# Scores of one head pair beside the running sums from chunk 3 on, in a single-core attention and MLP kernel with a written-out order

## The chip, the core and the metric

The kernel runs on one core of a Trainium2 chip. The metric is the device time of one execution in microseconds (us). In this text PE is TensorE, DVE is VectorE, ACT is ScalarE, POOL is GpSimd and SP is SyncE, the engine that issues most of the DMAs. PSUM is the memory that PE writes its results to; it has banks of 512 fp32 numbers in each of 128 partitions.

## The reference

Everything is float32, with batch B = 4, heads H = 8, sequence S = 768 and head size D = 48. First a gated recurrence, then a layer norm and a two-layer MLP with a residual:

```python
for t in range(S):
    state = alpha[:, :, t, :, None] * state + einsum('bhd,bhe->bhde', k[:, :, t], v[:, :, t])
    y[:, :, t] = einsum('bhd,bhde->bhe', q[:, :, t], state)
...
x = y.transpose(0, 2, 1, 3).reshape(B, S, 384)
xn = (x - mean(x)) / sqrt(var(x) + 1e-06) * g_ln
out = x + maximum(xn @ w_ch1, 0.0) @ w_ch2          # 384 -> 1536 -> 384
```

The three inputs of the MLP arrive on the chip as 64-bit floats and are rounded to float32 there, by DVE and ACT.

## The kernel before

**Work items.** The sequence is cut into six chunks of 128 steps. One item is one chunk `c` of one batch `b`, with all eight heads, held as four pairs `p` of two heads `i`. The generator `attention(c, b)` computes one item, from loads to the normalised and transposed rows of the MLP's input:

- ACT takes the logarithm of alpha into `la` (L308). PE multiplies it by a triangle of ones to get running sums of the logarithms, in the first 384 columns `lps[:, :DM]` of a PSUM bank (chunk 0 at L313; later by `running_sums`, L288, for most items ahead of time at L403, among the scores of an earlier item). ACT takes exponentials of them (L320, L321), and DVE multiplies keys and queries by those (L323, L325).
- DVE transposes them in blocks (L362), and DMAs through DRAM (`tr`, `td`) bring the transposed keys and queries `kT` and `qT`.
- Scores: PE multiplies `kT` and `qT` (L401), 64 x 64 for each head and each half `s` of the chunk. DVE copies the scores that a triangular mask lets through into `at` (`copy_predicated`, L413).
- State: PE multiplies keys and values into `sums` (L428); DVE adds the old state (L441) and POOL multiplies by the gate (L443), once for each half of the chunk: the tile `mid`, then `st`, which the next chunk of the same batch reads.
- Output `y`: PE adds what comes from the state (L459) and from the scores (L463) in two PSUM banks `yps`. ACT copies one to `x` (L486), DVE adds the other and sums the row for the mean (L489).
- ACT does the layer norm in several short steps (L502 to L515); PE transposes `xn` (L522), and ACT copies that to `xT` (L524). For the last two chunks DMAs do the transposes. The row `x` goes to DRAM for the residual (L498) and comes back later in `ob` (L545).

**The split.** For chunks from `SPLIT` on, the scores of pair 3 go to other places than those of pairs 0 to 2: into the last 128 columns of the bank that holds another item's running sums (`beside`, L389), and in each of the two halves of partitions that the other pairs leave free at that time. So there are two masked copies of 384 and 128 columns, pair 3's part of `y` lands in the opposite banks, and assembling `x` takes two copies by ACT (L474, L476) and two sums by DVE (L479, L482); the mean is made by L502 instead of L504, and `vx`, the values with their halves exchanged, is loaded in three parts instead of two (L153). The matmuls are the same in number and size.

**The MLP.** Chunk 0 is multiplied plainly (`hidden` L558, `project` L570). For chunks 1 to 5 both layers are done with fewer block products than blocks: 15 for the first layer (`hidden_product`, PE at L848, taken out of PSUM by DVE, ACT and POOL at L856 to L891) and 20 for the second (`product`, PE at L674, taken out at L684 to L734). Sums of blocks that these products need are made by DVE (`combine_first`, `combine_weights` L634, `combine_x` L825, `combine_hidden` L661).

**The order.** Nothing is scheduled by a planner. Each of these parts is a Python generator, and a `yield` ends one step of it. The string `ORDER` (L33) gives, letter by letter, which generator takes its next step:

```python
for turn in ORDER:
    next(turns[turn], None)
```

The letters `a` to `x` are the items, four to a chunk in the order of the batches, so `a` to `d` are chunk 0, `m` to `p` chunk 3, `q` to `t` chunk 4 and `u` to `x` chunk 5. `A` to `L` round the weights; `Y`, `Z`, `P` and `Q` are the MLP of chunk 0; `1` and `2` are the first layer's block products, `M` the second layer's, `N`, `S`, `W` and `X` the sums of blocks, `R` and `U` the relus, `O` the loads of rows back. Every engine executes what it was given in this order, and semaphores, which are set by the framework from the tiles that are read and written, hold an instruction until what it needs is there. Six PSUM banks (tag `bank`) serve scores, running sums, `yps`, transposes and products in turn.

Of the kernel before, what the change touches and what calls it, by code (L numbers as in the profile page):

```python
# [19 lines left out]
STAGED = 3  # L20
BY_DMA = 2
X_BY_DMA = 4
SPLIT = 4
AHEAD = 2
G = 32
SCORES = ((0, 0), (0, 1), (1, 0), (1, 1), (3, 0), (2, 0), (3, 1), (2, 1))
# [4 lines left out]


ORDER = (  # L33
    "bacabcadaacbcaadbcadabcababbebaccbadbaaBbccaedcbceAeeaaacbfecfBcdafddeaedbdeafae"
    "bcdccbfgadhAdcgCcdbebeebfhggdfgbfffbCdcgfgecdfchgdfhgabcddchdhAiiegjhacehedhhjfg"
    "biAdfidAeBhBijffYYiCjZZYYifZYlZCgjYDlYYjjZZYBZYgDieEgDgDjZZekEhZYGZgZigZGeeYgYgg"
    "fZYEhfGfkChihiYFYijfgEhgkhFZYhgYfghijgkFeZZlGZShfZYHlhHfYFYZeZHelYiZgllPmZkJIgJk"
    "PeiYjJIflHeSZIQgkIlYSjiPkffennSQlOKjLSnSjmSQhKnSjLnKPkiljnhSQnLkkjkWknkShOmPhkhl"
    "kOOhWlmmphmQmkmXjWQnXjlSQjPmkilXSXkP2OXWjXQjkjW2iXoSWX2oWX22Pi2mnol1j1mom2omSpoo"
    "l1XSpk2oW2m112p1m2pm11m1W211pp12O122r22jnn21lpnmnjSml1riOn2l12Rl111kqS1m21W1Rkp2"  # L40
    "o21mUXpq1mU2rUrnmj1rl2Rno2oomqonrormpokO1rNM2Mipin1op1ionoqUM2qp2W12RkMmNqiMoRtk"
    "UrpkqNM1NoMliMlNUMMNMNMKNqMlNorMWrnmtltNRMsqppMWNMriMMMpNlsqqqnoqttNttMtMsXMMssM"
    "sMNMNMX1oXXppMvstM2MXMMNMsppXoMXoqMsMMXM1nqqv11Xq1trMq2tqX21rn12v1r2ur2r222rvsqs"
    "svsu1rs1nuvvt2s11ss11p22rtsvosn2uropuXru222221uts212stnU1211u1121222Op1Rp2tRU21R"
    "Us1pXqU11x2tO2MM1vwMUM12xuRvu1vurNNNNwtOuuMwRxvNtxRNutwwMM2MOwNXwMNuXMMtNM1rMMMw"
    "qtXMMMxNUNxtMMsNMMMxXxMtXtrMMqMNrMXNvutMMwNuMMMNMMMxMLMOM11vvuq2X2O2wMus1wX11222"
    "2r2Xt1222w22utsqxvw2x2ww1vx21sX12121xwvq2O2x2w111u1uvU121w12s1wuRvx12U11J1q21R1U"
    "OvRxU121wMMu2xxsRNMw2NNMRM1MUNN2MMuUMqXN1MrNNRMNvMXNXMMMM2MMMxNM1uNXMMNMNMOXMXMv"
    "MMXOMMMXxNxwxMMvNMMMMMXMx21w1x222212v12w222x122w2212X11UX2212121121121wx111MU11X"
    "2RR2v1211212211R1URU211XOUM2XNRX1MX1RM2MXN2MXNXNMXXMXMMMN111U1MN1M1122MNM1MM2MM1"  # L50
    "11NNN121O11NM1MM21N1112N1122M1MMM12MM12N222M22M2RM1M2N22MM2MU1ON2M22M2UURR22RNNM"
    "MNM1MMOMRMNMUUM2ONMNNNMO2MMMUMNMMMMMRMMNNMMMNMNMMNMMMMMMMMNMNMMMMMMM"
)


# [1 line left out]
def kernel(  # L57
# [68 lines left out]
    def load(c, m, names):  # L126
# [12 lines left out]
        if "v" in names:  # L139
# [4 lines left out]
            if c:  # L144
# [4 lines left out]
                parts = ((0, 0, NP, NP), (1, 0, NP, 0))  # L149
                if c >= SPLIT:  # L150
                    parts = ((0, 0, NP, NP - 1), (1, 0, NP - 1, 0), (1, NP - 1, 1, H - 1))
# [142 lines left out]
    def attention(c, b):  # L294


        whole, last = c == 0, c + 1 == NCB
        split = c >= SPLIT
        if whole and b % 2 == 0:
# [660 lines left out]
```

## Time and profile before

| what | value |
|---|---|
| median of 3 runs | 421.56 us (421.01 to 423.45) |
| profiled execution | 420.14 us |
| its span (first to last instruction) | 418.3 us |
| PE busy | 409.8 us, 98% |
| DVE busy | 351.4 us, 84% |
| ACT busy | 177.5 us, 42% |
| POOL busy | 151.6 us, 36% |
| bytes moved by DMA | 61.26 MB, 146 GB/s in the mean |
| granted clock of PE | 1.00 |

The times of single lines come from the profiled execution, whose span lies 1.8 us below its own time and whose time lies 1.4 us below the median. A busy share is a mean over the whole span: whether an engine has room has to be read from windows. An engine's busy time counts instructions, which can overlap one another at their ends, so the distance from start to start can be less than a duration.

### The profile page before, as it was taken

Reading aid. Unit: us, or ns where it says so; the run is one execution under the profiler, and the core shown is the slowest. Engines: PE = TensorE matmul, PEld = TensorE weight load, DVE = VectorE, ACT = ScalarE, POOL = GpSimd, SP = SyncE. Lnnn points to the kernel's source line nnn. Section 1 sums busy time; section 2 is a strip of 40 time slices with the busy share of each in tenths; the row PEclk is TensorE's granted clock in tenths of the full one; section 3 lists DMA queues with packets and bytes.
Section 4 is the critical chain, followed back from the end, with each engine's and each line's share of the span. In section 5 each row is a group of like instructions: output and inputs, shape, how many; then the busy total and the mean of one; then the engine's idle time right before and its main releaser. Section 6 shows DMA issues by size and latency. Waiting matters only on the chain.

```text
span 418.3 us, 11560 instructions
## 1 busy us (share of the span) xinstructions
PE 409.8 (98%) x4608; PEld 361.3 (86%) x4608; DVE 351.4 (84%) x713; ACT 177.5 (42%) x440; POOL 151.6 (36%) x164
## 2 busy tenths in 40 slices
PE   7998999999999999999999999999999999999996
PEld 5787888766578889998889999889998899999996
DVE  4999999999999989996888995688876767977873
ACT  5598447724243496414546603364313242014110
POOL 1011000003203980043395033493152940499123
PEclk9999999999999999999999999999999999999999
DMA  8999999987888778587684546433035200001201
GB/s 278 340 302 288 235 196 306 270 184 195 193 233 175 207 153 193 123 203 179 135 213 85 130 102 162 88 96 78 0 116 102 67 0 2 1 19 40 94 20 56
DMA packets 135037, 61.26 MB, mean 146 GB/s; under 512 B 90908, under 2 KB 131100, under 8 KB 134984
## 3 DMA queue, kind: packets, MB, share of 16 engines
q1 hardware_dynamic: 134440, 60.37, 56.1%
q8 instruction: 36, 0.59, 0.6%
q10 hardware_dynamic: 544, 0.17, 0.2%
q14 instruction: 17, 0.14, 0.1%
HBM read 43.12 MB, written 17.39 MB: 145 GB/s over the span
## 4 chain that ended last, share of the span: by engine, by line
PE 89%; DVE 4%; DMA 2%; ACT 2%; issue 1%; POOL 0%; POOLq 0%; SPq 0%; DVEq 0%
PE hps L848 31%; PE ops L674 30%; PE ops L570 8%; PE hps L558 7%; PE aps L401 3%; PE yps L459 2%; PE yps L463 2%; PE sums L428 2%; DMA vn<-in_v_dram 2%; PE xps L522 1%; PE aps L393 1%; DMA ra<-in_alpha_dram 1%; PE lps L313 1%; DVE w L217 1%; PE tps L351 1%
## 5 line engine op out<-in xcount | busy, mean ns | idle before, releaser
L690 POOL TENSOR_TENSOR ob<-ob,u 128x192 f32<-128x192 f32 x40 | 26.2, 665 | 64.5 <-DVE ob L687 48.3
L848 PE MATMUL hps<-sum,w 128*128 128x256 f32 x192 | 46.3, 381 | 0.0
L898 ACT ACTIVATE hT<-hT 128x512 f32<-128x512 f32 x48 | 28.7, 622 | 35.0 <-POOL hT L870 18.5
L443 POOL TENSOR_TENSOR mid<-mid,gate 112x192 f32<-112x192 f32 x20 | 11.6, 580 | 81.8 <-DVE mid L441 51.3
L674 PE MATMUL ops<-w,hT 128*128 128x192 f32 x224 | 40.5, 327 | 0.0
L848 PEld LDWEIGHTS hps<-sum,w 128*128 128x128 f32 x192 | 36.1, 190 | 5.0
L674 PEld LDWEIGHTS ops<-w,hT 128*128 128x128 f32 x224 | 37.1, 190 | 0.7 <-issue 0.2
L848 PE MATMUL hps<-xT,w 128*128 128x256 f32 x136 | 34.0, 380 | 0.0
L570 PE MATMUL ops<-w,hT 128*128 128x384 f32 x96 | 33.0, 492 | 0.0
L558 PE MATMUL hps<-xT,w 128*128 128x256 f32 x144 | 32.5, 382 | 0.0
L558 PEld LDWEIGHTS hps<-xT,w 128*128 128x128 f32 x144 | 27.0, 190 | 4.2
L674 PE MATMUL ops<-ws,sum 128*128 128x192 f32 x160 | 28.7, 327 | 0.0
L848 PEld LDWEIGHTS hps<-xT,w 128*128 128x128 f32 x136 | 25.5, 190 | 3.1
L570 PEld LDWEIGHTS ops<-w,hT 128*128 128x128 f32 x96 | 17.5, 190 | 10.8 <-DVE w L232 0.4
L674 PEld LDWEIGHTS ops<-ws,sum 128*128 128x128 f32 x160 | 26.5, 190 | 0.3
L684 DVE TENSOR_TENSOR ob<-ops,ob 128x192 f32<-128x192 f32 x50 | 17.2, 351 | 10.6 <-PE ops L674 6.5
L443 POOL TENSOR_TENSOR st<-st,gate 112x192 f32<-112x192 f32 x16 | 11.6, 725 | 35.6 <-DVE st L441 25.9
L674 PE MATMUL ops<-ws,hT 128*128 128x192 f32 x128 | 23.6, 328 | 0.0
L459 PEld LDWEIGHTS yps<-st,qT 48*64 48x64 f32 x320 | 19.9, 134 | 4.0 <-issue 2.3
L463 PE MATMUL yps<-vx,at 64*64 64x48 f32 x320 | 22.7, 219 | 0.0
L401 PEld LDWEIGHTS aps<-qT,kT 48*64 48x64 f32 x576 | 19.1, 134 | 4.1 <-issue 0.8
L459 PE MATMUL yps<-st,qT 48*64 48x48 f32 x320 | 22.0, 220 | 0.6 <-ACT x L486 0.6
(248 smaller groups left out, 1131.6 us busy)
## 6 DMA issues: line engine op xcount, KB each, us to landing
ws<-in_moe_w_ch_dram SPq DMA_DIRECT2D x12, 768.0 KB, 5.8
td<-tr SPq DMA_DIRECT2D x64, 96.0 KB, 2.8
vn<-in_v_dram SPq DMA_DIRECT2D x12, 384.0 KB, 6.9
kept<-x SPq DMA_DIRECT2D x24, 192.0 KB, 3.0
ob<-kept SPq DMA_DIRECT2D x24, 192.0 KB, 3.0
out_dram<-ob SPq DMA_DIRECT2D x19, 192.0 KB, 1.9
ra<-in_alpha_dram SPq DMA_DIRECT2D x16, 192.0 KB, 2.6
kT<-td SPq DMA_DIRECT2D x32, 96.0 KB, 3.4
```

Source lines behind the costliest of these rows:

```text
L401: nc.tensor.matmul(to, kT[rs, p, s], qT[rs, p, s], start=True, stop=True)
L428: nc.tensor.matmul(up[h, p], qk_of(c, b)[ts, 1, p, i, :h.stop - h.start], vn[ts, i, p], start=True, stop=True)
L443: nc.gpsimd.tensor_mul(new, new, by)
L459: nc.tensor.matmul(yps[i][halves[s], i, p], qT[rs, p, s], (now, mid)[s][rs, p], start=True, stop=r != i)
L463: nc.tensor.matmul(yps[r][halves[s], i, p], at[halves[r], p, s], by, start=r != i, stop=True)
L558: nc.tensor.matmul(hps, w1[:, j // 2, f, j % 2 * P:][:, :P], xT_of[0][:, f, bs], start=(f == 0), stop=(f == NF - 1))
L570: nc.tensor.matmul(ops_of[b], hT_of[c][:, j, b], w2[:, j], start=(j == 0), stop=(j == NJ - 1))
L674: nc.tensor.matmul(acc, lhs[:, j], rhs[:, j], start=(j == 0), stop=(j == NT - 1))
L684: nc.vector.tensor_add(x, acc, x)
L690: getattr(nc.gpsimd, f"tensor_{op}")(x, x, y)
L848: nc.tensor.matmul(acc[:, i], w, b, start=True, stop=True)
L898: nc.scalar.activation(out=x, in_=x, func=AFT.Relu)
```

## The change

`SPLIT` goes from 4 to 3, so the four items `m` to `p` of chunk 3 are split like those of chunks 4 and 5, and the string `ORDER` is another one from its first letters on, with each letter as often as before. The instructions that come and go: four more masked copies on DVE (L413, 384 and 128 columns in place of 512), four more sums on DVE (L479 and L482 in place of L489), four more copies on ACT (L474 and L476 in place of L486), four L502 in place of L504, and two more loads of `vx`. Matmuls and bytes stay the same.

The diff, with the string cut to the first and last lines that change and those where chunk 3 is worked on:

```diff
@@ -20,7 +20,7 @@
 STAGED = 3
 BY_DMA = 2
 X_BY_DMA = 4
-SPLIT = 4
+SPLIT = 3
 AHEAD = 2
...
 ORDER = (
-    "bacabcadaacbcaadbcadabcababbebaccbadbaaBbccaedcbceAeeaaacbfecfBcdafddeaedbdeafae"
...
-    "kOOhWlmmphmQmkmXjWQnXjlSQjPmkilXSXkP2OXWjXQjkjW2iXoSWX2oWX22Pi2mnol1j1mom2omSpoo"
-    "l1XSpk2oW2m112p1m2pm11m1W211pp12O122r22jnn21lpnmnjSml1riOn2l12Rl111kqS1m21W1Rkp2"
-    "o21mUXpq1mU2rUrnmj1rl2Rno2oomqonrormpokO1rNM2Mipin1op1ionoqUM2qp2W12RkMmNqiMoRtk"
-    "UrpkqNM1NoMliMlNUMMNMNMKNqMlNorMWrnmtltNRMsqppMWNMriMMMpNlsqqqnoqttNttMtMsXMMssM"
...
-    "MNM1MMOMRMNMUUM2ONMNNNMO2MMMUMNMMMMMRMMNNMMMNMNMMNMMMMMMMMNMNMMMMMMM"
+    "abcbacaacdacdabababacbcaabcdadbcbcccbecabaaaedebbaefcafBadbedcefdbadeefcegdbgfdB"
...
+    "kWOlkWOlQmpSXmimiPmWXmlXPkpiQnookjSSXQPSX1jmiSXkS1Xklk1jXKW2Wj22QXW1jSjjk11mnOm1"
+    "oWn2lm2opoo2o2olnmj2mpm1il212Wp22l2122pj12W12pki1O2kmimUmjmn1p2Xnn1kq112ok1n2nk1"
+    "2XlO1m1q2irp122112m2opllRRUWorUpmR1o2MrrqrNrUUi1im2rllo2pMrM1otMl1RooRMpnNMlqqNp"
+    "1UNpMoqqnMN1omNtMplMnNpqpMNoMMNWpmrRMNoMsWOMqMNMMn2moMmrNqsNortqqqt1tMnttsssoqXt"
...
+    "MOMMMNR2RUNMMRMNUMNNNNMMMMMMMMN2MUMMMNOMNMNMMNMMMMMMNMMMNMMMMNMMMMMM"
 )
```

The code that the new value of `SPLIT` reaches in chunk 3 is L150 to L151 (loads of `vx`), L383 to L389, L397 to L404 and L412 to L416 (scores and their copies), L458 to L464 (`y`), L470 to L492 (`x`) and L501 to L504 (the mean).

More of the change, by code (lines that the diff above doesn't have):

```diff
@@ L33 @@
 ORDER = (
-    "bacabcadaacbcaadbcadabcababbebaccbadbaaBbccaedcbceAeeaaacbfecfBcdafddeaedbdeafae"
[L35 to L38, printed above, removed]
-    "kOOhWlmmphmQmkmXjWQnXjlSQjPmkilXSXkP2OXWjXQjkjW2iXoSWX2oWX22Pi2mnol1j1mom2omSpoo"
@@ L40 @@
-    "l1XSpk2oW2m112p1m2pm11m1W211pp12O122r22jnn21lpnmnjSml1riOn2l12Rl111kqS1m21W1Rkp2"
-    "o21mUXpq1mU2rUrnmj1rl2Rno2oomqonrormpokO1rNM2Mipin1op1ionoqUM2qp2W12RkMmNqiMoRtk"
-    "UrpkqNM1NoMliMlNUMMNMNMKNqMlNorMWrnmtltNRMsqppMWNMriMMMpNlsqqqnoqttNttMtMsXMMssM"
-    "sMNMNMX1oXXppMvstM2MXMMNMsppXoMXoqMsMMXM1nqqv11Xq1trMq2tqX21rn12v1r2ur2r222rvsqs"
-    "svsu1rs1nuvvt2s11ss11p22rtsvosn2uropuXru222221uts212stnU1211u1121222Op1Rp2tRU21R"
-    "Us1pXqU11x2tO2MM1vwMUM12xuRvu1vurNNNNwtOuuMwRxvNtxRNutwwMM2MOwNXwMNuXMMtNM1rMMMw"
@@ L46 @@
[L46 to L51, printed above, removed]
@@ L52 @@
-    "MNM1MMOMRMNMUUM2ONMNNNMO2MMMUMNMMMMMRMMNNMMMNMNMMNMMMMMMMMNMNMMMMMMM"
+    "abcbacaacdacdabababacbcaabcdadbcbcccbecabaaaedebbaefcafBadbedcefdbadeefcegdbgfdB"
+    "edecaaabcgdcACbagdghcbffgbhcffdecgdfgfgAcCbahcddddbchhbgdiAefihchdafjhhgebhcidBA"
+    "CdhYeiYZgljZjBeieZiYiCAYfZZejffgBYjYjjfkZYhDfYYEDDgfiYjfegEZDZYiEYZgYgZeZfglZhkh"
+    "giGCghZGeZggYjhhfeYZiEiZZgFjFGfiheYYeZlefYFYFjHYHSlYYkZlHlfhkeilnIhGhZZfYZIPiYeS"
+    "kfSlHZmSIJISkgfeZQlkSjQkgmgJJiPSOgQhgLLlhjhKLjlnkKnPnjQnKhSnPnOWkjSimkhjkkkPhnhS"
@@ new lines @@
+    "kWOlkWOlQmpSXmimiPmWXmlXPkpiQnookjSSXQPSX1jmiSXkS1Xklk1jXKW2Wj22QXW1jSjjk11mnOm1"
+    "oWn2lm2opoo2o2olnmj2mpm1il212Wp22l2122pj12W12pki1O2kmimUmjmn1p2Xnn1kq112ok1n2nk1"
+    "2XlO1m1q2irp122112m2opllRRUWorUpmR1o2MrrqrNrUUi1im2rllo2pMrM1otMl1RooRMpnNMlqqNp"
+    "1UNpMoqqnMN1omNtMplMnNpqpMNoMMNWpmrRMNoMsWOMqMNMMn2moMmrNqsNortqqqt1tMnttsssoqXt"
+    "MMsrMMNMpXMMtMvMXNNMMXqXMvsqMsMoXqpMXMXMoM21212qrq1tXts22v1M11r21r1vv2r2qu2p2rrs"
+    "qnnuO2s1psvrsus22Xn1vs1qt1r2Os211112s11vnp2ts1nXuus1uu21ssp2wU1ORU1o11221q2Rx1u2"
@@ new lines @@
+    "x122p122RvtR2UMMupttUOsoRMNMMXNMN2UNs2tNMrtwMuuMqNRutuvwqMUwwNvNMMMXMxxNXMMtNMus"
+    "NMNurwMvtMMMMXwMNxNxqrvuwMXNvwMsMuMMuNMMMMxXtMxM1XvXMMMM2OX2tM2t2twv21s1w112vvO2"
+    "21x21rv2112ru2X212qu12wXxOw1221w1wr21t1x1221xO2t211tuUs12xwRv111UU1RR12wMM211M22"
+    "wMMN1RNwMUNRN2UM1rMwMMrNMRxN2MsNqMNMNuwMNXMMUXMNXw1NwMMMMMvwNMxXMMXMNxvwMMMJXMNN"
+    "xMXM2MMuMMMM1XuX22v2x1Xx2M21Xx2Ox21v21222121222u2x2121x1w21111112x1212Rv11RuU2OU"
+    "11v21UR122xU111xXMMM2XX12M12X2MUX21RRXXXX1NMM2OO1MUN112R2MNN1M11NMMN11M111NM22X1"
@@ L53 @@
+    "1MNNM21MML1MN111NM2N2X2N1MM1MM1MN111M2O22MM12MM222UM2RN12RM222O2R2MNMUUMMN1122M2"
+    "MOMMMNR2RUNMMRMNUMNNNNMMMMMMMMN2MUMMMNOMNMNMMNMMMMMMNMMMNMMMMNMMMMMM"
 )
```

## Prediction

> **What bounds the kernel now.** I read the page first, then the table of waits of PE, the windows, the groups with their shapes kept apart, and the timelines of DVE and ACT. From the page: PE's busy time, PE and DVE in slices, the chain by engine.
>
> ```profile
> PE 409.8 (98%) x4608; PEld 361.3 (86%) x4608; DVE 351.4 (84%) x713; ACT 177.5 (42%) x440; POOL 151.6 (36%) x164
> ...
> PE   7998999999999999999999999999999999999996
> ...
> DVE  4999999999999989996888995688876767977873
> ...
> PE 89%; DVE 4%; DMA 2%; ACT 2%; issue 1%; POOL 0%; POOLq 0%; SPq 0%; DVEq 0%
> ```
>
> PE is the bound, but for half the span DVE is nearly full beside it. What PE waits for (engine and line that released it; us in total, times, longest):
>
> ```profile
> PE lps L313 <- ACT la L308: 1.6, 2, 1.4
> PE xps L522 <- DVE xn L511: 1.5, 1, 1.5
> PE lps L250 <- DVE more L247: 1.1, 1, 1.1
> PE yps L459 <- ACT x L486: 0.6, 1, 0.6
> PE sums L428 <- DVE st L441: 0.2, 1, 0.2
> ```
>
> And windows (busy us of PE, PEld, DVE, ACT, POOL with instructions, then clock, DMA share, GB/s) from 100 us on, where chunk 3 lies:
>
> ```profile
> 100.00:120.00 20.00, 19.38 (x338) 12.97 (x337) 19.53 (x37) 5.16 (x14) 3.37 (x4) 1.00 0.83 190
> 120.00:140.00 20.00, 20.00 (x334) 17.28 (x333) 18.91 (x36) 8.24 (x19) 8.36 (x9) 1.00 0.88 210
> 140.00:160.00 20.00, 19.93 (x337) 17.16 (x336) 18.32 (x37) 14.84 (x39) 15.00 (x14) 1.00 0.72 174
> ```
>
> After the start PE loses almost nothing, with DVE busy 18.3 to 19.5 us of each 20. So the question is whether dependent work still arrives in time.
>
> For that I add up a ledger: in the order in which each built program queues its instructions, the time each held its engine in this trace (start to next start, idle taken off). PE's queue holds 407.6 us before and, as its matmuls are the same 2,360, also after (switches between full-array and small matmuls, which cost it 93 ns in and about 135 ns out, go from 33 to 34). Start time minus work queued ahead is PE's idle time so far: 4.7 us at 40 us, 6.1 at 130, 6.6 at 185, 7.55 from 300 to the last matmul's end at 415.15. Only 2.9 us are lost after 40 us; with 0.2 in the tail and a part of the 1.5 us stall near 32 us, no new order can win more than about 3.5 us.
>
> **Part one, the split for chunk 3.** The groups (out<-in, shapes, count | busy us, mean ns | idle ahead):
>
> ```profile
> L413 DVE COPY_PREDICATED at<-consts,aps 128x512 f32<-128x512 int32 x12 | 8.7, 724 | 0.4 <-PE aps L401 0.4
> ...
> L489 DVE SCALAR_TENSOR_TENSOR x<-yps,x 128x384 f32<-128x384 f32 x12 | 6.6, 549 | 0.4 <-ACT x L486 0.4
> ...
> L413 DVE COPY_PREDICATED at<-consts,aps 128x384 f32<-128x384 int32 x8 | 4.7, 587 | 4.3 <-PE aps L401 3.7 <-PE lps L401 0.7
> ...
> L479 DVE SCALAR_TENSOR_TENSOR yps<-x,small 128x96 f32<-128x96 f32 x8 | 3.8, 478 | 0.0
> L482 DVE SCALAR_TENSOR_TENSOR x<-yps,x 128x288 f32<-128x288 f32 x8 | 3.7, 458 | 0.3
> ...
> L474 ACT ACTIVATE x<-yps 128x336 f32<-128x336 f32 x8 | 3.6, 448 | 17.4 <-PE yps L463 9.4 <-DVE xr L528 8.0
> ...
> L413 DVE COPY_PREDICATED at<-consts,lps 128x128 f32<-128x128 int32 x8 | 2.3, 286 | 0.0
> ```
>
> - DVE, four items (one a batch). By row means 587+286-724 = 0.15 us and 478+458-549 = 0.39 us, 0.54 each, 2.1 us in all. Instructions overlap at their ends, so start to next start is the truer price: .48+.19 for the two copies against .62, and about .35+.35 for the two sums with their accumulator reads against .48. That is 0.27 each, +1.1 us of DVE queue. I take 1.1 and keep 2.1 as the end; this work hides beside PE only as far as DVE has room.
> - ACT: 448+206 for 485, and L502 at 282 for L504 at 200: 0.25 us each, 1.0 us on a 42% engine.
> - PE: a score block (36 matmuls, first to last start) took 930 ns unsplit, 904, 896, 903 and 963 split; a y block (64) took 930 and 945 to 1089 (mean 1009). Net +0.065 an item, +0.26 us; I take +0.1, since some of the long y blocks may be waits.
> - SP: two more loads of vx (L153) behind the others on its queue; vx is used by the y block, and its bytes stay the same. I take 0; transposed keys of chunk 3, which leave in that queue, landed at 143.96 us for a use at 145.4, so late loads would cost up to 1 us.
>
> The Trainium skill, "TensorEngine Tiling (Array Packing)", Theoretical Speedup, gives up to 2x for dimensions of at most 64, with four independent 64x64 tiles. The split puts a quarter of the small matmuls on the two quadrants that the others leave idle; if that ran wholly beside them, both blocks would shrink by a quarter, and by it the sum would lose 4 x 0.46 = 1.9 us of PE. The split blocks of chunk 4 in this trace show -14 ns and +79 ns instead, so the trace decides against it.
>
> **Part two, the new order.** Here I compare the ledgers.
>
> 1. *DVE ahead of PE.* For each PE instruction that waits for DVE: PE work queued before it minus DVE work up to its producer. Before, the smallest in 120 to 140 us is 1.6 us; after, -0.1: n's update (L428) at PE work 131.9 waits for m's state (L441) at DVE work 132.0. Counted from chunk 0's third item, whose update releases DVE (L437) at PE work 22.7 and DVE work 18.5, PE has 109.2 us to that place and DVE 113.5. So PE must idle about 4.3 us over this stretch, which the order of before needed only to 2.4 us (2.7 measured). PE's offset there becomes 6.5 to 6.8 instead of 6.1: +0.4 to +0.7, taken +0.55. What is late next is everything after it, one for one.
> 2. *ACT in strict order, 156 to 167 us of PE work.* (A) The second bank of p's y block (L463) is free once o's first copy (L474) is done. On ACT that stands behind the copy of product 15 (L693), whose last matmul (L674) stands right ahead of p's y block on PE. PE has nothing to do meanwhile: last matmul 0.163 + start of ACT 0.037 + to the next start 0.215 + L474 0.448 + start of PE 0.054 = 0.92 us. In the order of before no copy stands like this. (B) r's running sums (L403) wait for ACT's copy of m's transposes (L524, row 471 ns), and those transposes (L522) are right ahead on PE: 0.17 + 0.04 + 0.48 + 0.05, less 0.07 of work between, 0.67 us. (C) The next product (L674) waits for l's L524, behind the copy L721 of the product before it and two short activations: about 0.35 us. Together +1.94 us. From below: 0, if PE reaches the spot late because of step 1 and ACT's earlier work is done (the waits of A and B are PE to ACT to PE and do not shrink by that, so I lean to the full price); from above, +1.94 and 0.5 us for a DVE transfer they push back.
> 3. *What is taken away.* The stall of 0.62 us near 114 us is inside the 6.1 of step 1. The small ones from 130 to 190 us, 0.44 together, stand elsewhere in the new order: -0.4. At the end DVE waits 1.29 us at 410.34, then runs two sums L661 (DVE's timeline: start, duration):
>
> ```profile
> 410.34 0.36 DVE L684 TENSOR_TENSOR ob<-ops,ob 128x192 f32<-128x192 f32 x1 [1.29 <-ACT u L734]
> 410.62 0.68 DVE L661 TENSOR_TENSOR sum<-sum,at 128x512 f32<-128x512 f32 x1
> 411.33 0.69 DVE L661 TENSOR_TENSOR sum<-sum,sum 128x512 f32<-128x512 f32 x1
> ```
>
> The new order puts the first of them into that gap, so the POOL chain behind L684 ends 0.6 us sooner, and the last L684, which waits 1.10 us for POOL, waits for the last matmul instead: -0.2.
>
> Sum: 0.1 + 0.55 + 1.94 - 0.4 - 0.2 = +2.0 us. On the profiled execution's 420.14 us (span 418.3 and 1.8 around it) that is 422.1; the runs' median is 1.42 above it, so 423.6.
>
> **The rivals.**
>
> - *The waits dissolve.* Steps 1 and 2 cost under half: A to C overlap one another or the offset. For it: PE had 0.62 us of such waits before, and they were few. Against it: each is written in the queues. 0.1 + 0.3 + 0.6 - 0.6 = +0.4: about 422.0.
> - *Faster.* The new order has every producer ahead of PE from 100 us on: the stalls of before go (0.62 at 114 us, 0.44 to 185 us, the 1.0 from there to 300 us, 0.2 in the tail, 0.3 at the start) and A to C do not appear: about -2.5 us, 419.1. It decides from the point where steps 1 and 2 together cost under 0.4 us. Against it: step 1 has DVE with 1.9 us less room than before.
> - *DVE becomes the bound of chunk 3.* With the 2.1 us price and waits on ACT and POOL inside DVE's own queue, its 19.5 busy of 20 has no room: +2.0 and 2 to 3 more, about 426. The Trainium skill's page above, PSUM Bottleneck, speaks for it: packing speeds up TensorE but not the evacuation of its results. Here the evacuation is the two copies and two sums at +0.27 us, and DVE was already at 95%.
> - *The split pays on PE.* If a quarter of the small matmuls ran beside the rest, -1.9 us would cancel the sum: 421.7. Against it stand the blocks of chunk 4 above.
>
> **How the numbers follow.** This kernel's runs spread by 0.6%, and 0.5% (2.1 us) is about what a measurement can tell. The sum as it stands: 0.52, half of it on each side of 423.7. Waits dissolve 0.15 and packing pays 0.03 (no change). DVE-bound 0.18 and late loads 0.02 (slower). Faster 0.10, of which 0.08 beyond 2.1 us. So slower 0.26+0.18+0.02 = 0.46, faster 0.08, no change 0.26+0.18+0.02 = 0.46. The range leaves out most of the faster case and the far end of the DVE-bound one: 420.0 to 428.0.
>
> **What would show it.** The table of waits after should list PE yps L463 <- ACT x L474 near 0.9 us, PE lps L403 or its bank <- ACT xT L524 near 0.7, and PE sums L428 <- DVE st L441 near 0.5, all between 120 and 175 us; PE's offset should be 8.5 to 9.5 at its end instead of 7.55, DVE's busy time 1 to 2 us up, and the tail's POOL wait gone. It is wrong if PE's idle time from 120 to 175 us is under 0.8 us, if the waits lie elsewhere, or if PE's own blocks in chunk 3 change by over 0.1 us.

## The result, and the profile after

The changed kernel took 425.28 us in the median of six runs (424.66 to 426.83), the kernel before 421.54 us in six (420.53 to 423.45): a ratio of 1.0086 with a 95% interval of 1.0057 to 1.0114. The prediction was 423.6 us, between 420.0 and 428.0. So it is slower, on the side the sum pointed to, and by 3.7 us instead of 2.0.

The profiled execution took 425.28 us, with a span of 423.5. The page of after: PE's busy time and the chain by engine.

```profile
PE 413.1 (98%) x4608; PEld 362.8 (86%) x4608; DVE 355.7 (84%) x725; ACT 179.4 (42%) x444; POOL 149.1 (35%) x164
...
PE 89%; DVE 5%; DMA 3%; issue 1%; ACT 1%; POOL 0%; SPq 0%; DVEq 0%; POOLq 0%; ACTq 0%
```

The shares hardly differ from before. The table of waits of PE does:

```profile
PE xps L522 <- DVE xn L511: 2.0, 1, 2.0
...
PE tps L351 <- DVE qk L325: 0.9, 1, 0.9
PE yps L463 <- ACT xT L524: 0.6, 1, 0.6
PE hps L848 <- DVE x L482: 0.5, 1, 0.5
PE yps L463 <- ACT x L474: 0.5, 1, 0.5
...
PE ops L674 <- DVE ob L684: 0.3, 1, 0.3
PE lps L403 <- ACT xT L524: 0.3, 1, 0.3
PE hps L848 <- DVE hT L882: 0.3, 1, 0.3
```

Of the five waits of before two are gone (behind L486 and L441), one has shrunk (behind L308, from 1.6 to 0.4), one has grown (behind L511, from 1.5 to 2.0), and seven new ones have come. The table counts only the time in which PE shows no work at all, and a matmul's end is modelled. So I use the measure of the prediction, start time minus work queued ahead, with the durations of before. PE's idle time so far, in us, by the time in the trace:

| trace time, us | 60 | 130 | 150 | 180 | 200 | 240 | end |
|---|---|---|---|---|---|---|---|
| before | 4.67 | 6.10 | 6.36 | 6.57 | 6.88 | 7.23 | 7.55 |
| after | 6.02 | 6.45 | 7.30 | 9.49 | 9.95 | 12.36 | 12.90 |
| order alone | 6.64 | 6.92 | 7.84 | 10.04 | 10.51 | 12.92 | 13.46 |
| three waits taken away | 5.62 | 6.23 | 7.10 | 7.68 | 8.10 | 10.69 | 11.23 |
| six waits taken away | 6.26 | 6.69 | 6.80 | 7.41 | 8.50 | 9.35 | 9.88 |

The loss comes in steps. The largest are 150 to 180 us (+2.2 after against +0.2 before), where the prediction had put its three waits, and 200 to 240 us (+2.4 against +0.35), where it had put nothing. ACT's timeline of after shows the first group at its source (start, duration, instruction, idle ahead):

```profile
162.79 0.32 ACT L721 COPY u<-ops 128x192 f32<-128x192 f32 x1 [2.12 <-PE ops L674]
...
163.44 0.46 ACT L524 COPY xT<-xps 128x384 f32<-128x384 f32 x1
165.56 0.32 ACT L693 COPY u<-ops 128x192 f32<-128x192 f32 x1 [1.66 <-PE ops L674]
165.78 0.46 ACT L474 ACTIVATE x<-yps 128x336 f32<-128x336 f32 x1
```

ACT is idle for 2.12 and for 1.66 us because the copy at the head of its queue waits for a product of PE; the copy behind it (L524, L474), whose data had been there since 160.6 and 163.9 us, is the one that PE needs next. The product behind L524 starts at 163.96, and the matmuls of p's y block into the second bank, behind L474, at 166.29.

The last DVE instruction starts 0.11 us after PE's last matmul ends (0.27 before): the tail's wait for POOL is gone, as forecast.

### The profile page after: what moved, and what is told of

Same layout as the page of the kernel before. It is cut to its first block, busy times and chain, and to the rows that moved or that the text cites. A ratio compares the mean times of both kernels' runs of the same rounds, so it can differ in the third digit from the quotient of the medians.

```text
span 423.5 us, 11570 instructions
## 1 busy us (share of the span) xinstructions
PE 413.1 (98%) x4608; PEld 362.8 (86%) x4608; DVE 355.7 (84%) x725; ACT 179.4 (42%) x444; POOL 149.1 (35%) x164
## 4 chain that ended last, share of the span: by engine, by line
PE 89%; DVE 5%; DMA 3%; issue 1%; ACT 1%; POOL 0%; SPq 0%; DVEq 0%; POOLq 0%; ACTq 0%
PE ops L674 31%; PE hps L848 28%; PE hps L558 8%; PE ops L570 8%; PE aps L401 3%; PE yps L459 2%; PE sums L428 2%; PE yps L463 2%; DMA rq<-in_q_dram 1%; PE tps L351 1%; PE aps L393 1%; PE xps L522 1%; DMA ra<-in_alpha_dram 1%; PE yps L454 1%; PE lps L401 1%
## 5 line engine op out<-in xcount | busy, mean ns | idle before, releaser
L443 POOL TENSOR_TENSOR mid<-mid,gate 112x192 f32<-112x192 f32 x20 | 13.0, 652 | 88.1 <-DVE mid L441 84.6
L684 DVE TENSOR_TENSOR ob<-ops,ob 128x192 f32<-128x192 f32 x50 | 17.4, 352 | 15.7 <-PE ops L674 6.9
L463 PE MATMUL yps<-vn,at 64*64 64x48 f32 x320 | 22.6, 220 | 0.0
L401 PE MATMUL aps<-qT,kT 48*64 48x64 f32 x544 | 22.2, 225 | 0.0
L674 PE MATMUL ops<-more,sum 128*128 128x192 f32 x120 | 22.1, 327 | 0.0
```

The costliest lines, as they stand in the source:

```text
L401: nc.tensor.matmul(to, kT[rs, p, s], qT[rs, p, s], start=True, stop=True)
L443: nc.gpsimd.tensor_mul(new, new, by)
L463: nc.tensor.matmul(yps[r][halves[s], i, p], at[halves[r], p, s], by, start=r != i, stop=True)
L674: nc.tensor.matmul(acc, lhs[:, j], rhs[:, j], start=(j == 0), stop=(j == NT - 1))
L684: nc.vector.tensor_add(x, acc, x)
```

## The experiments

My theory ahead of them: the new order writes waits into the queues, and these are the loss. The rivals: the split's own work on DVE is the loss, or waits that are taken away come back behind DVE. Each ratio below is against executions of before that ran beside it, whose median was between 421.0 and 421.8 us; a range in us has that much room.

**1. The order without the split, and the split without the order.**

```diff
 # the new ORDER            # the old ORDER
-SPLIT = 3                  -SPLIT = 4
+SPLIT = 4                  +SPLIT = 3
```

> The new order with SPLIT back at 4. Theory (T): the time after went into waits that the new order itself writes into the queues (PE behind ACT at 138, 164, 166 and 176 us, PE behind DVE at 219 to 220 and 234 to 238 us, 4.2 us together, and 1.2 us more at the start); without the split they all stay, and only the split's own price leaves: 0.26 us of PE and up to 1.1 us of DVE. So 424.3 to 425.2 us against 425.3 after. Rival (R1): the split's work on DVE in chunk 3 is what costs; then this kernel is within 1 us of before, 421.0 to 422.5.

Measured: 426.22 us against 421.83 of before, 1.0091 (1.0070 to 1.0111). The order alone costs all of the change's loss. From 60 us to the end it lost 6.82 us of PE, the order with the split 6.88: within the new order the split costs 0.06 us, not the 0.4 to 1.4 that the theory still had kept for it; the time lies 1.0 us above T's range. R1, which allowed at most 422.5, fell.

> The order of before with SPLIT at 3. T: the split costs little by itself, but its copies and sums stand in an order that leaves DVE 1.6 us of room there, so +0.5 to +2.5 us: 422.0 to 424.0, with new waits of PE between 120 and 180 us. R1 (the split costs nearly all): 424.5 to 426.0. If it costs nothing: 421.5.

Measured: 425.34 us, 1.0067 (1.0043 to 1.0091), above T's range of 422.0 to 424.0 and inside the one that was written for R1. One of its windows (busy us of PE, PEld, DVE, ACT, POOL) and five lines of its table of waits, all from 150 to 160 us, show where:

```profile
150.00:160.00 10.00, 6.83 (x179) 5.42 (x179) 8.58 (x17) 5.88 (x17) 6.41 (x6) 1.00 0.50 133
```

```profile
PE lps L403 <- ACT xT L524: 0.9, 1, 0.9
...
PE lps L403 <- DVE hT L882: 0.7, 1, 0.7
PE ops L674 <- DVE at L413: 0.7, 1, 0.7
...
PE hps L848 <- DVE sum L825: 0.6, 1, 0.6
PE yps L463 <- DVE at L413: 0.3, 1, 0.3
```

PE loses 3.2 of the ten us after 150, 2.3 of them behind DVE and 0.9 behind ACT, and its idle time by the measure above goes from 10.66 to 15.05 there; in before it went from 6.2 to 6.4 over the same work. So the same split costs nothing that shows in one order, and in the other 4 us in this trace and about 3 by the ratio. It fits the rival "DVE becomes the bound of chunk 3", for an order that wasn't made for the split. But DVE, at 8.58 of ten us, is no fuller here than in before over the same work (8.59 from 145 to 155), so that the split's DVE work pushes these waits up is argued and not shown. The rest of this kernel's profile can't be compared: its profiled execution, 428.65 us, is the slowest of its seven and had lost 3.8 us more than before already by 60 us.

**2. Three waits taken away, then six.** Turns are written as letter and step, with steps counted from 0 (150 is step 50 of the generator `1`).

```diff
-... n18 M7 N4 ... M8 p15 l26 M9 ... p17 M10 N7 o18 M11 ...
+... n18 l26 M7 N4 ... M8 p15 o18 M9 ... p17 M10 N7 M11 ...
-... M17 M18 n20 ... m25 o20 M19 m26 r9 ...
+... M17 m25 m26 M18 n20 ... o20 M19 r9 ...
```

> After, with three moves of one step or two each, that take away what the three forecast waits of PE on ACT stand behind: o's copies (L474) ahead of product 15's copy (L693), l's copy to xT (L524) ahead of product 14's copy (L721), m's transposes and their copy (L522, L524) one product earlier. T: PE's waits at 163.96, 166.29 and 175.93 us go (0.43, 0.82 and 0.63), nothing takes their place: -1.9 us, 423.4. Rival (R2): DVE is the bound of these stages, the waits come back behind DVE: -0.5 us at most, 424.8.

Measured: 424.54 us, 1.0049 (1.0031 to 1.0067). PE's idle time grew by 0.6 us instead of 2.2 between 150 and 180, and by 1.67 less to the end. The waits for L474 and of L403 for ACT's L524 have left the table, and what lies behind is unchanged (the same waits at 217 to 236 us, of the same length). In this trace nothing took their place, which speaks against R2. The times decide less: the ratio fell by 0.37%, 1.6 us, but the intervals of the two kernels overlap, and the median lies nearer to R2's 424.8 than to T's 423.4.

```diff
-... U0 m17 j26 m18 ...
+... m17 j26 U0 m18 ...
-... u3 u4 s18 150 u5 u6 248 151 s19 ...
+... u3 s18 150 248 151 s19 u4 u5 u6 ...
-... N19 s22 260 t16 N20 M46 r20 t17 w1 M47 ... w2 q24 M49 ...
+... s22 260 t16 M46 r20 t17 w1 M47 N19 N20 ... M49 w2 q24 ...
```

> As the kernel with three moves, and three more places: the first relu of half 1 (L898) behind j's copy to xT (L524), two steps of item u (L325, L362) behind s's sums (L479, L482), and around products 11 and 15 of chunk 2 two sums of blocks (L661) and w's exponentials (L320, L321) behind the copies and additions that PE waits for. T: the waits at 138, 218.6 to 220.3 and 234.3 to 237.6 us go too (0.9, 1.1, 0.9), less 0.3 for a wait on DVE that stands right behind the first: -4.5 us, 420.8, about the time of before. R2: half of it comes back as waits on DVE: 423.

Measured: 422.10 us, 1.0002 (0.9984 to 1.0020): level with before. This is what is left in its table of waits:

```profile
PE xps L522 <- DVE xn L511: 2.0, 1, 2.0
PE tps L351 <- DVE qk L325: 1.1, 1, 1.1
PE lps L250 <- DVE more L247: 1.1, 1, 1.1
PE hps L848 <- issue: 0.4, 1, 0.4
PE lps L313 <- ACT la L308: 0.3, 1, 0.3
```

All but the fourth lie in the first 35 us. The six waits are thus shown to be the loss in the time, by taking them away: by the ratios 0.84% of 421.8, 3.5 us of the 3.7. I had expected 4.5, and R2 half of it. Of PE's idle time 3.0 of the 5.35 us by which after exceeds before have gone; the other 2.3 still stand between this trace and before's, which was one of before's faster executions. About 1.2 us stayed or came back: between 193 and 198 us PE loses 1.1, where after lost 0.46 from 180 to 200, and between 228 and 235 it loses 0.8, partly in waits for L684 that were only shortened. What makes the loss at 193 to 198 is not settled; the profile names "issue" for 0.4 of it.

**3. The same without the split.** The edit of experiment 2 with SPLIT at 4.

> The kernel with six waits removed, with SPLIT back at 4: what the split is worth in an order without these waits. T: it costs PE 0.26 us and DVE 1.1 us that hide: this kernel is 0 to 0.6 us faster than with the split, 421.5 to 422.1. Rival: the order was made for the split, and without it new waits appear: 422.6 or more. If the split gains (packing): 424.

Measured: 421.06 us against 421.37 of before, 0.9998 (0.9973 to 1.0023); with the split it was 1.0002. The time lies below T's range, far from both other cases. In an order free of these waits the split is worth nothing that shows, in either direction.

**4. Is the start bound by DVE?**

```diff
-... A1 c21 C1 b20 ... b21 c23 h3 h4 b22 ...
+... A1 c21 b20 ... b21 c23 C1 h3 h4 b22 ...
```

> After, with one step moved: the second set of rounding instructions (C's first step, L215 to L219, about 2.1 us of DVE) stands behind the normalisations of b and c (L511) instead of ahead of them, so that the wait of PE at 32.8 us (2.0 us, transposes of b for L511) loses its cause. Theory (T): DVE is the bound of the first 130 us (PE must idle about 4.3 us between the update of chunk 0's third item and n's update, wherever), so the wait comes back at the next step that DVE owes (h's L325), PE's idle time at 130 us stays at 6.3 to 7.2 us and the time at 425.0 to 426.1. Rival (R): the wait is the order's own and goes: -1.2 us or more, 424.1 or less.

Measured: 427.02 us, 1.0129 (1.0096 to 1.0161). The wait came back one step on, as T said, and larger (the first line):

```profile
PE tps L351 <- DVE more L325: 2.5, 1, 2.5
PE tps L351 <- DVE qk L325: 1.8, 1, 1.8
...
PE xps L522 <- DVE xn L511: 0.7, 1, 0.7
```

R fell. But T's size fell too: the kernel lost 1.7 us instead of up to 0.8, and PE's idle time at 130 us was 7.9, not 6.3 to 7.2. Not all of that 7.9 belongs to the move: the second line lies at 9.8 us, ahead of it, where after waited 0.9 us and the profiled executions of experiment 2 1.4 and 1.1 for the same instruction. The times show that an order can stand above the floor of 4.3 us; by how much, this trace doesn't say.

**5. Two waits of the old order taken away.**

```diff
-... k17 i17 l14 X2 S11 X3 k18 P6 20 ...        -... M187 M188 M189 M190 M191 N78 M192 ...
+... k17 k18 P6 i17 l14 X2 S11 X3 20 ...        +... M187 N78 M188 M189 M190 M191 M192 ...
```

> Before, with three letters moved: k's copy (L486) and one product of chunk 0 (L570) ahead of i's y block, which waited 0.62 us for that copy at 114 us, and one sum of blocks (L661) two products earlier, ahead of the gap of 1.29 us of DVE at 410 us. T: 0.6 and 0.1 to 0.2 us less: 421.0 against 421.8 of before, and no wait of PE on L486 in the table of waits. Rival: DVE, at 19.5 of 20 us there, takes the 0.6 back within the next 30 us: 421.6. This run is also a second look at the start of the old order: PE's idle time at 40 us was 4.7 us in the profile of before, 8.4 with the split alone.

Measured: 420.56 us against 421.37 in the medians, but 0.9997 (0.9967 to 1.0028), since four of its twelve runs lay between 421.8 and 425.7: not told apart from before. In the table of waits L486 is gone, and a line that before did not have has come:

```profile
PE aps L401 <- DMA qT<-td: 0.4, 1, 0.4
```

PE reached m's scores sooner, found the transposed queries of the second half not yet there (they landed at 121.84 us) and went on at 121.97. So 0.4 of the 0.6 us was given back within 8 us, to a DMA and not to DVE as the rival had it. The start is as in the profile of before, 4.9 us of idle time at 40 us.

**6. The clock behind PE's wait at 31 us.** In after PE stands idle for 2.0 us there, and the windows of after (the column behind the busy times is the granted clock) show what follows:

```profile
30.00:34.00 4.00, 2.00 (x13) 1.26 (x11) 3.93 (x9) 3.87 (x15) 0.00 (x0) 0.92 1.05 372
34.00:36.00 2.00, 1.85 (x9) 1.54 (x8) 2.00 (x6) 1.92 (x5) 0.00 (x0) 0.50 0.85 250
36.00:38.00 2.00, 2.00 (x71) 1.90 (x71) 1.97 (x4) 1.25 (x3) 0.00 (x0) 0.80 1.01 222
```

The clock is at half for about 3.4 us. An execution with such a dip has a mean of 0.996 or less. I filled the wait with 14 matmuls of zeros in the first two kernels and 10 ahead of another turn in the third (`spare` is 128 unused columns of a bank of `sums`):

```diff
+            for _ in range(14 if n == POSITION else 0):     # ahead of turn b22
+                nc.tensor.matmul(spare, zero, zero, start=True, stop=True)
             next(turns[turn], None)
```

> After, with 14 matmuls of zeros (128x128, results unused) put on PE's queue where it waits 2.0 us at 30.8 us. In the executions of after whose mean granted clock is 0.996 (4 of 6) the profile shows the clock at 0.5 from about 33.4 to 36.8 us, behind that wait; the executions at 1.0 were 0.7 us faster (424.7 against 425.4). Theory (C): the clock falls because PE stood idle that long. Then the fillers keep it up: 1.0 in nearly all executions, and the median at 424.6 to 424.8. Rival: the dip has nothing to do with PE's idle time; then as many executions as before are at 0.996, and the median stays at 425.3 or rises by the fillers' time.

> The kernel with six waits removed (10 of its 12 executions at 0.996, 422.3; the two at 1.0 421.2), with the same fillers. Theory (C): all at 1.0, median 421.1 to 421.3, 0.5 us below before's 421.4 to 421.8. Rival: as for the kernel above, 422.1.

> Before with its two waits taken away (9 of 12 executions at 1.0, 420.5; 3 at 0.996, 422.8), with 10 such matmuls where PE waits 1.5 us at 32.4 us. Theory (C): all at 1.0 and a median of 420.4 to 420.6, 0.2% below before. Rival: as often at 0.996 as without.

Measured: the clock was at 0.999 or 1.0 in all 6 and all 12 executions of the first two, where 4 of 6 and 10 of 12 had dipped. So the idle time makes the dip. But the times were 425.80 (1.0107), 422.35 (1.0030) and 423.33 us (1.0062; here one of twelve still dipped): not better, and for the third clearly worse. Fourteen fillers took 3.29 us, twice my estimate, and held b's transposes back by a microsecond. So with eight:

> After with 8 matmuls of zeros instead of 14: with 14 the clock stayed at 1.0 in all 6 executions, but they took 3.3 us (0.22 us each, twice what was assumed) and held b's transposes back until 33.8 us. Eight take 1.75 us and end ahead of 32.8 us. Theory (C): clock 1.0 throughout and the time of the executions of after without the dip, 424.6 to 424.9. Rival: the dip costs nothing that PE doesn't wait for anyway, since DVE is late there: 425.3 as after.

> The kernel with six waits removed, with 8 such matmuls. Theory (C): clock 1.0 throughout, 421.1 to 421.4 (its two executions without the dip were at 421.2), level with before. Rival: 422.1 to 422.3, as with the dip.

Measured: the clock at 0.999 or 1.0 in all 18, and 425.16 us (1.0097; 1.0077 to 1.0118) and 421.54 us (1.0008; 0.9993 to 1.0023). Against 1.0086 and 1.0002 without fillers nothing is gained. (In us the second lies 0.14 above theory C's range, but before ran faster beside it too, at 421.18.) The windows of after with eight fillers show what takes the place of the dip:

```profile
34.00:36.00 2.00, 1.59 (x15) 1.10 (x13) 2.00 (x6) 2.00 (x6) 0.00 (x0) 1.00 1.03 335
36.00:38.00 2.00, 1.84 (x69) 1.66 (x67) 1.97 (x5) 1.82 (x5) 0.00 (x0) 1.00 0.88 163
```

At full clock PE has gaps there, 1.59 of 2 us and 1.84 of 2, with DVE and ACT both at 2.00 in the first: it waits 0.41 us for ACT (L222) and 0.16 for DVE in the time that the slow clock would have used. So filling the wait gains nothing here, and theory C is shown only on what causes the dip. That the dip itself costs nothing is not shown: within one kernel the executions with it were slower, 425.4 against 424.7 us in after and 422.3 against 421.2 with the six waits taken away, and what else differs in them is open.

No version beat both kernels beyond its interval.

## Why the prediction was right, and where its sum was short

**What bounds the kernel.** Right. PE is at 98% in both, and the difference is PE's idle time: 12.90 against 7.55 us, 5.35, which is the difference of the spans (5.2) to 0.17, the part that the tail won. The page counts 3.3 us of it as busy time (413.1 against 409.8) though the matmuls are the same: their ends are modelled, and where the clock is at half (experiment 6) the transposes of L351 start 0.21 us apart instead of 0.11.

**The split's prices.** The switch to more small matmuls, the fuller DVE and the longer ACT cost 0.06 us together in the new order, where I had taken 0.1. The DVE work of the split hid. DVE's busy time rose by 4.3 us instead of 1 to 2, but the order alone has 355.0 of the 355.7 us: 3.6 of the 4.3 are the new order's, in which for example the sums L661 of two running sums take 838 ns in the mean instead of 716. Packing gained nothing: two y blocks of chunk 3 that run without a wait took 943 and 978 ns with the split and 895 and 930 in the order alone, so the trace's verdict on the rule of the Trainium skill stands. That the cover can go, the split alone in the old order shows.

**Step 1, DVE ahead of PE.** Forecast: an offset of 6.5 to 6.8 instead of 6.1 near 130 us. Measured 6.45: +0.35 for +0.55. The stall itself was not at L428 but earlier, at the start, from where the offset of 6.0 was carried. So the place was wrong, and the size is no proof: with the same start, the profiled executions of order alone and of experiment 2 stood at 6.92, 6.23 and 6.69 there.

**Step 2, three waits behind ACT.** Forecast 0.92, 0.67 and 0.35; the steps in PE's idle time at 166.29, 175.93 and 163.96 us were 0.82, 0.63 and 0.43. The sum, 1.88 for 1.94, was nearly exact, and taking them away gave 1.67. The third was smaller than its step says: from the product at 161.29 to the one at 163.96 PE took 2.67 us, and 2.52 with the waits taken away, so 0.15 us is the wait's. The first two lean on no estimate of a load: a copy that waits for PE at the head of ACT's queue, and PE waiting for the copy behind it, can be written down from the order and four row durations.

**Step 3, what is taken away.** This term failed: -0.4 for the small stalls of before. The stall at 114 us is gone, and the tail came out at -0.17 for -0.2. But of the small ones the new order has its own, 0.46 us from 180 to 200.

**What the sum did not have.** Three places, by the steps of the idle time there:

- 0.8 us at 138.15. j's copy L524, whose transposes were done at 134.67, stood behind a relu that waited for POOL:

```profile
137.10 0.63 ACT L898 ACTIVATE hT<-hT 128x512 f32<-128x512 f32 x1 [2.20 <-POOL hT L870]
137.64 0.46 ACT L524 COPY xT<-xps 128x384 f32<-128x384 f32 x1
```

  I had searched for copies behind waits for PE; this wait is for POOL, which waits for DVE, which waits for PE.
- 1.1 us at 218.62 and 220.28, where products wait for DVE's L882 and L482; 0.9 us at 234.32 and 237.63, where they wait for L684 behind sums of blocks and behind a copy of ACT. All of this lies in the work of chunks 4 and 5. The prediction's step 2 ended at 167 us of PE work, where the split's new part ends; the new order is new everywhere.

These three, 2.8 us, on top of the sum's 2.0 and the 0.4 that it took off in vain make 5.2 us, about the difference of the two profiled executions (5.1). The medians differ by 1.4 us less, because before's profiled execution, 420.14 us, lay 1.4 below its median of 421.54, while after's lay on its own. The prediction added that 1.42 to both, as if the excess were the same; for after it was nothing. So part of the miss in the mechanism was cancelled by the scale: that the measured 425.28 came within 1.7 us of the forecast is in part luck. What slows the other executions of before no trace here shows.

**The rivals.** "The waits dissolve" and "faster" didn't occur. "DVE becomes the bound of chunk 3" fits what the split did in the old order, not in the new. The tests named at the end of the prediction hold for L474 and L403 (0.5 and 0.3 in the table of waits, 0.82 and 0.63 by start times) and for the offset's direction (12.90, beyond its 8.5 to 9.5); the wait on L441 is not in the table. By its own sign "if the waits lie elsewhere" the prediction had about half of the loss in the wrong place.

## What to carry to other kernels

In an order written out by hand on engines that take their queue in order, look for the pair: an instruction that waits for engine X at the head of Y's queue, and behind it one that X needs next. Its price follows from a few rows, in this kernel it came on top of what was lost elsewhere, and moving one or two letters took it away; but search it through chains of three engines too, and over the whole span, not only where the change is. A busy engine beside the bound gives at most a floor for the idle time: whether the same extra work costs nothing that shows or 3 to 4 us was decided here by the order.

## What the runs showed of the hardware

**DVE can wait for POOL inside an instruction.** L479, 96 columns with both inputs in SBUF, took 252 to 266 ns when no POOL instruction was running as it started. Where one was, it took 375 to 957 ns in before and 382 and 1093 in after, in six of seven cases (at 146.3 us of after it was not held up), and ended 0.12 to 0.13 us after that instruction. The longest:

```profile
218.49 1.09 DVE L479 SCALAR_TENSOR_TENSOR yps<-x,small 128x96 f32<-128x96 f32 x1
```

```profile
218.19 1.26 POOL L874 TENSOR_TENSOR hT<-hT 128x512 f32<-128x512 f32 x1
```

L479 was 0.83 us longer here than alone, and PE's step of 0.70 us at 220.28, behind the L482 that follows, fits into that. L482, with one input in PSUM, took 457 or 458 ns in all 12 cases of after, POOL busy or not. The Trainium skill, "GPSIMD Engine Reference", Specifications, says that POOL shares its SBUF interfaces with VectorE and that they contend where a DVE instruction has two SBUF inputs; the trace agrees. The row mean of 478 ns that the prediction had was thus a mixture of two cases.

**An idle time of 2 us can halve the clock.** The dip of about 3.4 us behind PE's wait came in 4 of 6 executions of after and in none of the 18 with eight fillers. The Trainium skill, "TensorE: Matmul & The Clock Gate", What's actually happening, has the clock at half after a window of about 3.4 us of idleness, with windows that run freely. The length of the dip agrees; PE's idle gap was shorter than such a window, 2.0 us in one piece, and with the short gaps behind it PE was busy for 2.0 of the 4 us from 30 to 34.
